# Batch 3's local q and k by DMA transposes instead of matrix transposes, with batch 4's loads reordered, in a fused sparse-attention and squared-ReLU kernel

## The chip, the cores and the metric

The kernel runs on one core of one Trainium2 chip. The time is device microseconds of one execution of the whole program. A core has five engines that run side by side, each in its own program order: TensorE (PE, matrix work), VectorE (DVE), ScalarE (ACT), GpSimd (POOL) and SyncE (SP). Here POOL mainly issues the loads from memory, which also convert float32 to bfloat16, and SP issues the stores and the transposes that DMA engines make.

## The reference

Eight batches of attention with 8 heads, 576 positions and 64 dimensions per head. Heads 0 to 3 see the last 32 positions ("local"), heads 4 to 7 see the positions of the same remainder modulo 32 ("strided"). The output, 4608 rows of 512, goes through a two-layer network.

```python
scores = scale * np.matmul(q, k.transpose(0, 1, 3, 2))
mask_local = (rel >= 0) & (rel < stride)                       # stride = 32
mask_strided = (rel >= 0) & (pos[None, :] % stride == pos[:, None] % stride)
masks = np.stack([mask_local if h < H // 2 else mask_strided for h in range(H)], axis=0)
scores = np.where(masks[None, :, :, :], scores, -1000000000.0)
attn = np.exp(scores - np.max(scores, axis=-1, keepdims=True))
attn = attn / (np.sum(attn, axis=-1, keepdims=True) + 1e-09)
attn_out = np.matmul(attn, v)
x = np.ascontiguousarray(attn_out.transpose(0, 2, 1, 3)).reshape(B * S, H * D)
out = np.square(np.maximum(x @ w_in, 0.0)) @ w_out
```

## The kernel before

**Tiles.** A unit is two heads of one batch, numbered 4 x batch + pair. Units 0 and 1 of a batch (so 12 and 13 for batch 3) are local, the other two strided. A local unit works on six tiles of 96 queries with 128 keys each, the 32 keys before the tile and its own 96. The attention result stands transposed in `xt` (four tiles of 128 x 4608). The network runs over nine chunks of 512 rows: first layer `mm1` (L709, 16 groups of four matmuls a chunk), relu on ScalarE (L715), square on VectorE (L716), second layer `mm2` (L731, 16 groups a chunk), copy to `y` (L735) and a store by SP (L739).

**Order.** The order is written by hand. The network's groups are numbered from 0, and `PLAN` lists, for each group, the steps of attention that are issued just ahead of it. Each engine takes its part of the steps in that order. Batch 3's attention is spread over groups 19 to 85, batch 4's over 40 to 121. Group 48 is the first of the second layer of chunk 1, group 64 the first of the first layer of chunk 2, group 80 the first of its second layer.

**Steps of the local units.** `l` loads the float32 rows of two units into the unused end of `xt` in one DMA (`load_qk_local_sw`, L292). `c` copies them into bfloat16 tiles `q_l`, `k_l` (L299), on the engine that the last letter names (v VectorE, a ScalarE). `T` makes six transposes on TensorE into PSUM (L455) and copies them out (L462). `Q` instead loads one unit's rows straight into `q_l` or `k_l`, one DMA per head (`load_qk_rows`, L280), and `Y` transposes q and k with two DMA transposes on SP (`transpose_local`, L380). Before, batches 0 to 3 go by `l`, `c`, `T` (batch 0 by loads of its own), batches 4 to 7 by `Q`, `Y`. `S` (with `!`, all at once) makes the scores, four exponentials on ScalarE (L523) and two masks on VectorE (L529), the first mask one group later, the second two. `D` multiplies by V, one head per part (L669), and divides on VectorE (L674, L675). `E` transposes the result into `xt`, from batch 2 on by DMA on SP (L684). From batch 4 on both local units' scores are made together by `G` (L552, exponentials L563, masks L559).

**V of the local units.** `V` loads it (`load_v_local_all`, L420): 128 partitions, of which the first 32 hold the last 32 rows of the tile before, so that those rows are loaded twice. For batch 0 `load_v_local_sw` (L405) loads the 96 own rows alone and `H` (`shift_v_local`, L412) copies partitions 96 to 127 to 0 to 31 of the next tile.

**Steps of the strided units.** `C` loads q or k (L351) into one staging tile for each of the two names; `X` transposes it by DMA on SP (L356) into `qT_s` (two buffers) or `kT_s` (one buffer). `k` copies `kT_s` into the block-diagonal `kb` (L367, L370), `U` loads V (L392, L395), `B` copies it into the block-diagonal `vb` (L399). `s` makes scores (L576), exponentials (L577) and a mask (L579); `x` the row sums (L587) and products (L590), a logarithm and an exponential for the reciprocal (L592, L593), and the products on VectorE into `xt` (L600; L606 for the third part).

**Queues.** All loads above stand in POOL's one queue, all DMA transposes and stores in SP's; an instruction there that waits holds up what stands behind it. The staging tile of `C` is free again when its `X` has landed.

Of the kernel before, what the change touches and what calls it, by code (L numbers as in the profile page):

```python
# [38 lines left out]
19: C2q C2k V2 k11v D4.0  # L39
20: s1.0 D4.1 B10v  # L40
21: s1.1 D5.0
22: B11v l3k12+13 s1.2 U2
23: D5.1 x1.0
24: E4a
25: x1.1
26: X2k l3q12+13
27: x1.2
28: V3 E5a
29: c9kv
30: c8qv  # L50
31: c8ka c9qv X2q
# [1 line left out]
35: T8kv  # L53
37: T9kv
38: T8qv C3k
41: S8!
42: T9qa
44: S9! D8.0 k20v
45: D8.1 k21v
46: B20v  # L60
47: E8 D9.0 B21v U3
48: Q16k s2.0
49: D9.1
50: Q17q Q16q c12kv s2.1
51: c12qa E9 s2.2
52: Q17k c13kv c13qa
54: x2.0
55: X3q X3k
56: x2.1 C4k C4q
57: T12ka  # L70
58: V4 T13qv T12qa
59: T13ka
60: x2.2 B30v
61: B31v
63: U4 S12!
64: X4q
65: D12.0
66: Y17 k30v
67: Y16 D12.1 S13! X4k C5q k31v
68: C5k  # L80
71: s3.0 E12 Q20k Q21q Q20q
72: Q21k s3.1
73: D13.0 D13.1
75: E13
77: s3.2
80: x3.0 B40v
81: B41v
82: x3.1
85: x3.2
90: G4 k40v  # L90
91: k41v
95: U5 D16.0 D16.1
97: Y20
99: X5k
100: C6k
101: X5q
# [62 lines left out]
def kernel(  # L159
# [136 lines left out]
    def cast_qk_local(u, name, copy):  # L296
        s = st[u]
        t = qk_in.tile([QL, 6, 2, D], BF16, name=f"{name}_l")
        copy(t.rearrange("p j h d -> p h j d"), s[name + "f"].rearrange("p h (j d) -> p h j d", j=6))  # L299
        s[name] = t  # L300
# [16 lines left out]
    def step_TS(b, name, g, copy):  # L317
        src = str_rows[b, name]
        pt = bank("pt").bitcast(BF16)[:, 0:S]
        if b:  # L320
            for i in range(NJ):
                c = 128 * (NJ * g + i)
                nc.tensor.transpose(pt[:, SP_ * i:SP_ * (i + 1)], src[:, c:c + 128], ident[0:SP_, 0:SP_])
            if g == 0:
                o = strTs[name].tile([128, NP2 * SR], BF16, name=f"{name}T_s")
                str_T[b, name] = o.rearrange("c (a p) -> c a p", p=SR)
            copy(str_T[b, name][:, NJ * g:NJ * (g + 1), 0:SP_], pt.rearrange("c (a p) -> c a p", p=SP_))
            return
        for i in range(2):
            for s3 in range(NP3):  # L330
                c = 128 * (2 * g + i)
                o = S // 2 * i + QL * s3
                nc.tensor.transpose(pt[:, o:o + QL], src[:, s3, c:c + 128], ident[0:QL, 0:QL])
        if g == 0:
            o = strTs[name].tile([128, 2 * NJ * SR], BF16, name=f"{name}T_s")
            str_T[b, name] = o[:, 0:2 * NJ * SP_].rearrange("c (a r) -> c a r", a=NJ // 2)
        o = str_T[b, name]
        copy(o[:, 2 * g:2 * g + 2, :].rearrange("c a r -> c (a r)"), pt)
        if g == 1:
            for i in range(2):  # L340
                st.setdefault(2 + i, {})[name + "T"] = \
                    o[:, :, 2 * SP_ * i:2 * SP_ * (i + 1)].rearrange("c a (h p) -> c h a p", h=2)
# [71 lines left out]
    def load_v_local_all(b):  # L414
        i = (2 * b) % NV
        t = vl_all[:, i:i + 2]
        src = v[b - 1:b + 1].rearrange("b h s d -> (b h s) d")
        r0 = H * S - 32
        src = bass.AP(src.tensor, src.offset + r0 * D, [[D, 128], [QL * D, 4 * NL], [1, D]])
        nc.gpsimd.dma_start(out=t[:, :, :, :, 0:D].rearrange("p u h t d -> p (u h t) d"), in_=src)  # L420
        for u in range(2):
            st.setdefault(4 * b + u, {})["v"] = t[:, u]
# [27 lines left out]
    def step_T(u, name, copy):  # L450
        s = st[u]
        src = s[name].rearrange("p j h d -> p (j h d)")
        pt = bank("pt").bitcast(BF16)[:, 0:S]
        for j in range(6):
            nc.tensor.transpose(pt[:, QL * j:QL * (j + 1)], src[:, 128 * j:128 * (j + 1)],  # L455
                                ident[0:QL, 0:QL])
        if name == "k":
            full = kTl[v_slot(u)]
            dst = full[:, 32:32 + S]
        else:  # L460
            full = dst = qkT.tile([128, S], BF16, name="qT")
        copy(dst.rearrange("c (p j) -> c p j", j=6), pt.rearrange("c (j p) -> c p j", j=6))  # L462
        s[name + "T"] = full
# [79 lines left out]
    def step_G(b):  # L543

        us = (4 * b, 4 * b + 1)
        bk = [bank("pt") for _ in range(6)]
        bk = [bk[0::2], bk[1::2]]
        for t in range(2 * NL):
            for row in range(2):
                s, j = st[us[t // NL]], t % NL  # L550
                rows, c = slice(64 * row, 64 * row + 64), QL * (t % 4)
                nc.tensor.matmul(bk[row][t // 4][:, c:c + QL], s["kT"][rows, QL * j:QL * j + 128],  # L552
                                 s["qT"][rows, QL * j:QL * (j + 1)], start=True, stop=True)
        e = es01[:, 0:4 * S].rearrange("p (r c) -> p r c", r=2)

        def masks(row):
            x = e[:, row].rearrange("p (u t c) -> p u t c", u=2, c=QL)
            for i in range(2):
                nc.vector.tensor_tensor(x[:, i], x[:, i], mask_all, op=ALU.mult)  # L559

        for row in range(2):
            for i in range(3):
                nc.scalar.activation(e[:, row, 4 * QL * i:4 * QL * (i + 1)], bk[row][i][:, 0:4 * QL], AF.Exp, scale=scale)  # L563
            later(row + 2, lambda row=row: masks(row), ("G", b, row))
# [197 lines left out]
    def warm(n):  # L762
        if n:
            pw = bank("py")
            for _ in range(n):
                nc.tensor.matmul(pw, idle[:, 0:128], idle, start=True, stop=True)
# [7 lines left out]
    def run_step(word):  # L774
        word, _, at = word.partition("/")
        places[:] = [int(x) for x in at.split(",") if x]
        op, arg = word[0], word[1:]
        if op == "w":
            warm(int(arg))
        elif op == "c":  # L780
            cast_qk_local(int(arg[:-2]), arg[-2], ENG[arg[-1]])
        elif op == "T":
            step_T(int(arg[:-2]), arg[-2], ENG[arg[-1]])
        elif op == "W":
            step_TS(int(arg[0]), arg[1], int(arg[2]), ENG[arg[3]])
        elif op == "S":
            u, _, half = arg.rstrip("!").partition(".")
            step_S(int(u), int("!" in arg), [int(half)] if half else range(2))
        elif op == "G":
            step_G(int(arg))  # L790
        elif op == "b":
            step_B(*(int(x) for x in arg.split(".")))
        elif op == "N":
            step_N(int(arg))
        elif op == "O":
            step_O(int(arg))
        elif op in "sx":
            (step_SS if op == "s" else step_XX)(*(int(x) for x in arg.split(".")))
        elif op == "k":
            step_K(int(arg[0]), int(arg[1]), ENG[arg[2]])  # L800
        elif op == "m":
            memset_later(arg[:-1], nc.gpsimd if arg[-1] == "g" else nc.vector)
        elif op == "D":
            if "." in arg:
                u, part = arg.split(".")
                step_D(int(u), int(part))
            else:
                step_D0(int(arg))
        elif op == "E":
            step_E(int(arg.rstrip("av")), ENG.get(arg[-1]))  # L810
        elif op == "P":
            first_part(*([int(x) for x in y] for y in arg.split(".")))
        elif op == "H":
            shift_v_local(int(arg[:-1]), ENG[arg[-1]])
        elif op == "C":
            load_str_tall(int(arg[:-1]), arg[-1])
        elif op == "Q":
            load_qk_rows(int(arg[:-1]), arg[-1])
        elif op == "X":
            transpose_str(int(arg[:-1]), arg[-1])  # L820
        elif op == "Y":
            transpose_local(int(arg))
        elif op == "V":
            load_v_local_all(int(arg))
        elif op == "U":
            load_v_str(int(arg))
        elif op == "B":
            spread_v_str(int(arg[0]), int(arg[1]), ENG[arg[2]])
        elif op == "l":
            load_qk_local_sw(int(arg[0]), [int(x) for x in arg[2:].split("+")], arg[1])  # L830
        elif op == "r":
            load_str_rows(int(arg[0]), arg[1])
        elif op == "i":
            load_w_in(int(arg))
        elif op == "o":
            load_w_out(int(arg))
        elif op == "z":
            late_constants()
        else:
            raise ValueError(word)  # L840
# [143 lines left out]
```

## Time and profile before

| | us |
|---|---|
| median of 3 runs (301.0 to 301.94) | 301.18 |
| profiled execution | 300.84 |
| its span, first to last instruction | 299.1 |
| TensorE busy in the span | 292.6 |
| VectorE, ScalarE, GpSimd busy | 178.5, 172.7, 72.5 |
| granted TensorE clock | 1.00 throughout |

The page of the profile gives the busy time of each engine and its share over 40 slices of the span. The timeline lists instructions in order of time, those of one form that follow each other merged: start, length, engine, line, operation, what it writes and reads, how many, and in brackets how long the engine was idle before and what ended that. For SP the length is the time that it took to issue; a transfer lands later. The view of a tile or line gives the shortest, median and longest duration. The costliest groups are these (busy us, mean ns of one, idle time of the engine before them):

```profile
L709 PE MATMUL psb<-xt,w_in_b 128*128 128x512 bf16 x576 | 133.7, 379 | 0.8 <-ACT xt L694 0.4
L731 PE MATMUL psb<-w_out_b,g_sb 128*128 128x512 bf16 x560 | 128.2, 379 | 0.0
L715 ACT ACTIVATE r<-psb 128x512 bf16<-128x512 f32 x144 | 85.4, 599 | 38.2 <-PE psb L709 34.7
L716 DVE TENSOR_TENSOR g_sb<-r 128x512 bf16<-128x512 bf16 x144 | 60.9, 424 | 75.5 <-ACT r L715 74.6
```

### The profile page before, as it was taken

How to read it: one execution, taken by the hardware profiler on the slowest of the kernel's cores; microseconds unless marked ns; L12 is line 12 of the kernel's file. 1: busy time of each engine (PE TensorE's matmuls, PEld its weight loads, DVE VectorE, ACT ScalarE, POOL GpSimd, SP SyncE). 2: the span in 40 equal slices, each digit the busy share in tenths (PEclk: the TensorE clock that was granted, in tenths of full speed). 3: DMA queues.
4: the chain of work that ended last, by engine and by line, in shares of the span. 5: the costliest groups of instructions: out<-in, count | busy, mean ns of one | idle time of the engine just before them, and what ended most of it. 6: DMA issues, size and time to landing. Idle time of an engine off the chain costs nothing.

```text
span 299.1 us, 5688 instructions
## 1 busy us (share of the span) xinstructions
PE 292.6 (98%) x2172; PEld 146.4 (49%) x2172; DVE 178.5 (60%) x460; ACT 172.7 (58%) x325; POOL 72.5 (24%) x105
## 2 busy tenths in 40 slices
PE   7989999999999999999999999999999999999996
PEld 3654555545545445444454445444454444444444
DVE  5857699569678695589257945685485525104400
ACT  3758855786668744773467546645665356126511
POOL 8746743004604009056303720000000000000000
PEclk9999999999999999999999999999999999999999
DMA  7999999999999999999998998611011110010012
GB/s 148 189 210 202 184 200 189 153 227 110 144 141 192 171 161 190 151 153 135 192 174 141 159 188 136 110 56 71 35 23 44 67 51 0 35 72 36 0 70 72
DMA packets 93132, 37.28 MB, mean 125 GB/s; under 512 B 78957, under 2 KB 87239, under 8 KB 93105
## 3 DMA queue, kind: packets, MB, share of 16 engines
q0 software_dynamic: 54448, 18.82, 60.3%
q1 hardware_dynamic: 38512, 18.03, 31.6%
q8 instruction: 17, 0.28, 0.4%
q14 instruction: 11, 0.08, 0.1%
q10 hardware_dynamic: 144, 0.07, 0.1%
HBM read 38.21 MB, written 9.44 MB: 159 GB/s over the span
## 4 chain that ended last, share of the span: by engine, by line
PE 88%; ACT 4%; DMA 2%; DVE 2%; issue 2%; POOL 0%; DVEq 0%; ACTq 0%; POOLq 0%
PE psb L709 39%; PE psb L731 39%; DMA w_out_b<-in_k_dram 2%; PE psb L669 2%; PE psb L590 1%; ACT r L715 1%; PE psb L756 1%; PE psb L576 1%; PE psb L587 1%; ACT e L511 1%; PE psb L455 1%; PE psb L552 1%; PE psb L507 1%; DVE vb L399 1%; ACT qT L462 0%
## 5 line engine op out<-in xcount | busy, mean ns | idle before, releaser
L709 PE MATMUL psb<-xt,w_in_b 128*128 128x512 bf16 x576 | 133.7, 379 | 0.8 <-ACT xt L694 0.4
L731 PE MATMUL psb<-w_out_b,g_sb 128*128 128x512 bf16 x560 | 128.2, 379 | 0.0
L715 ACT ACTIVATE r<-psb 128x512 bf16<-128x512 f32 x144 | 85.4, 599 | 38.2 <-PE psb L709 34.7
L716 DVE TENSOR_TENSOR g_sb<-r 128x512 bf16<-128x512 bf16 x144 | 60.9, 424 | 75.5 <-ACT r L715 74.6
L709 PEld LDWEIGHTS <-w_in_b 128*128 128x128 bf16 x576 | 53.4, 98 | 59.3 <-issue 2.1
L731 PEld LDWEIGHTS <-g_sb 128*128 128x128 bf16 x560 | 51.7, 97 | 57.1 <-DVE g_sb L716 0.3
L735 ACT COPY y<-psb 128x512 f32<-128x512 f32 x35 | 20.7, 590 | 53.6 <-PE psb L731 53.5
L600 DVE TENSOR_TENSOR xt<-psb,rv 64x144 bf16<-64x144 f32 x84 | 34.1, 406 | 7.8 <-ACT rv L593 6.7
L592 ACT ACTIVATE rv<-psb 128x432 f32<-128x432 f32 (+1 forms) x21 | 10.5, 500 | 10.4 <-PE psb L587 10.4
L675 DVE TENSOR_TENSOR x_l<-psb,rinv 96x384 bf16<-96x384 f32 x28 | 15.5, 554 | 1.0
L351 POOL DMA_DIRECT2D q_t<-in_q_dram x6 | 3.4, 567 | 44.9 <-DMA qT_s<-q_t 42.7
L606 DVE TENSOR_TENSOR xt<-psb,rv 64x270 bf16<-64x270 f32 (+1 forms) x28 | 10.9, 432 | 3.7 <-ACT rv L593 3.5
L577 ACT ACTIVATE e<-psb 128x432 bf16<-128x432 f32 (+1 forms) x21 | 10.4, 496 | 3.7 <-PE psb L576 3.7
L280 POOL DMA_DIRECT2D k_l<-in_k_dram x16 | 11.9, 746 | 2.2 <-ACT rv L593 1.9
L420 POOL DMA_DIRECT2D vl<-in_v_dram x7 | 10.3, 1474 | 7.6 <-PE psb L552 3.7
L280 POOL DMA_DIRECT2D q_l<-in_q_dram x16 | 11.8, 742 | 0.0
L563 ACT ACTIVATE e<-psb 128x384 bf16<-128x384 f32 x24 | 9.6, 509 | 3.4 <-PE psb L552 3.4
L593 ACT ACTIVATE rv<-rv 128x432 f32<-128x432 f32 (+1 forms) x21 | 11.2, 533 | 0.7
L669 PEld LDWEIGHTS <-e 128*128 128x128 bf16 x168 | 8.6, 101 | 4.8
L559 DVE TENSOR_TENSOR e<-e,mask_all 128x576 bf16<-128x576 bf16 x16 | 6.7, 459 | 6.9 <-ACT e L563 6.8
L351 POOL DMA_DIRECT2D k_t<-in_k_dram x6 | 3.2, 538 | 28.0 <-DMA kT_s<-k_t 25.8
L669 PE MATMUL psb<-vl,e 128*128 128x65 bf16 x168 | 9.5, 195 | 0.0
(117 smaller groups left out, 217.4 us busy)
## 6 DMA issues: line engine op xcount, KB each, us to landing
out_dram<-y SPq DMA_DIRECT2D x35, 256.0 KB, 2.8
vl<-in_v_dram POOLq DMA_DIRECT2D x7, 384.0 KB, 11.4
w_out_b<-in_moe_w_out_dram POOLq DMA_DIRECT2D x4, 512.0 KB, 14.3
q_t<-in_q_dram POOLq DMA_DIRECT2D x7, 288.0 KB, 6.4
k_t<-in_k_dram POOLq DMA_DIRECT2D x7, 288.0 KB, 6.6
v_st<-in_v_dram POOLq DMA_DIRECT2D x7, 216.0 KB, 8.3
w_in_b<-in_moe_w_in_dram POOLq DMA_DIRECT2D x2, 704.0 KB, 14.0
k_l<-in_k_dram POOLq DMA_DIRECT2D x16, 72.0 KB, 7.1
```

The source lines that it names most:

```text
L280: nc.gpsimd.dma_start(out=t[:, :, hh, :], in_=src[b, 2 * p + hh].rearrange("(t p) d -> p t d", p=QL))
L592: nc.scalar.activation(rv, pn, AF.Ln)
L593: nc.scalar.activation(rv, rv, AF.Exp, scale=-1.0)
L600: nc.vector.tensor_tensor(to[:, :, NJ * part:NJ * (part + 1), par], of, by, op=ALU.mult)
L606: nc.vector.tensor_tensor(t, of[:, g:, :, lo:lo + k], by[:, g:, :, lo:lo + k], op=ALU.mult)
L669: nc.tensor.matmul(po[0:m, n, :], e[:, c:c + m], rhs[:, NL * part + n, 0:D + 1], start=True, stop=True)
L675: nc.vector.tensor_tensor(x, po[0:QL, :, 0:D], rinv[0:QL].to_broadcast([QL, NL, D]), op=ALU.mult)
L709: nc.tensor.matmul(ph, w_in_b[:, kk, 128 * ff:128 * (ff + 1)], xt[kk][:, 512 * c:512 * (c + 1)], start=(kk == order[0]), stop=(kk == order ...
L715: nc.scalar.activation(r, ph, AF.Relu)
L716: later(1, lambda: nc.vector.tensor_tensor(g[:, ff, :], r, r, op=ALU.mult))
L731: nc.tensor.matmul(py, g[:, ff, 128 * j:128 * (j + 1)], w_out_b[:, ff, :], start=(ff == 0), stop=(ff == 15))
L735: nc.scalar.copy(y, py)
```

## The change

Four things are edited in the plan, and one in the step that carries out `V`.

1. Units 12 and 13: `l3k12+13` and `l3q12+13` become `Q12k Q13k` and `Q12q Q13q` in the same places (22, 26); the casts at 50 to 52 and the `T` steps at 57 to 59 are gone; `Y12` comes at 40 and `Y13` at 52.
2. Batch 4: `Q16` and `Q17` move from 48 to 52 to 56, between the strided loads; `X4k` goes ahead of `Y17` and `Y16`; V4 and U4 move from 58 and 63 to 67, behind `C5q`.
3. V of batches 3 and 4 is loaded by `load_v_local_sw`, 96 partitions, and `H3v`, `H4v` copy the shared rows on VectorE.
4. Batch 3's strided steps s3, x3, k30v, k31v come up to two groups later, B40v and B41v move from 80 and 81 to 97 and 98.

```diff
-22: B11v l3k12+13 s1.2 U2
+22: B11v Q12k Q13k s1.2 U2
-26: X2k l3q12+13
+26: X2k Q12q Q13q
-28: V3 E5a
+28: E5a V3
+40: Y12
-48: Q16k s2.0
+48: s2.0
-50: Q17q Q16q c12kv s2.1
-51: c12qa E9 s2.2
-52: Q17k c13kv c13qa
+50: s2.1
+51: E9 s2.2
+52: Y13
-56: x2.1 C4k C4q
-57: T12ka
-58: V4 T13qv T12qa
-59: T13ka
+56: x2.1 C4q Q16k Q16q C4k Q17k Q17q
 60: x2.2 B30v
 61: B31v
-63: U4 S12!
+62: H3v
+63: S12!
 64: X4q
 65: D12.0
-66: Y17 k30v
-67: Y16 D12.1 S13! X4k C5q k31v
-68: C5k
-71: s3.0 E12 Q20k Q21q Q20q
-72: Q21k s3.1
-73: D13.0 D13.1
-75: E13
-77: s3.2
-80: x3.0 B40v
-81: B41v
-82: x3.1
+66: X4k Y17
+67: D12.1 S13! Y16 C5q V4 U4
+68: k30v
+69: k31v C5k
+71: E12 Q20k Q21q Q20q
+72: Q21k
+73: D13.0 D13.1 s3.0
+75: E13 s3.1
+78: s3.2
+81: x3.0
+83: x3.1
 85: x3.2
+94: H4v
 95: U5 D16.0 D16.1
-97: Y20
+97: Y20 B40v
+98: B41v
...
         elif op == "V":
-            load_v_local_all(int(arg))
+            (load_v_local_sw if int(arg) in (3, 4) else load_v_local_all)(int(arg))
```

The functions that it now calls for batches 3 and 4 stood in the kernel already:

```python
def load_v_local_sw(b):
    i = (2 * b) % NV
    t = vl_all[:, i:i + 2]
    nc.gpsimd.dma_start(out=t[32:128, :, :, :, 0:D].rearrange("p u h t d -> p (u h t) d"),
                        in_=v[b, 0:4].rearrange("h (t p) d -> p (h t) d", p=QL))

def shift_v_local(b, copy):
    t = vl_all[:, (2 * b) % NV:(2 * b) % NV + 2].rearrange("p u h t d -> p (u h) t d")
    copy(t[0:32, :, 1:NL, 0:D], t[96:128, :, 0:NL - 1, 0:D])
```

All other steps keep their places. Line numbers after the plan move by one.

## The prediction

> **What bounds the kernel now.** I read the page first: busy times, then slices.
>
> ```profile
> PE 292.6 (98%) x2172; PEld 146.4 (49%) x2172; DVE 178.5 (60%) x460; ACT 172.7 (58%) x325; POOL 72.5 (24%) x105
> PE   7989999999999999999999999999999999999996
> ```
>
> TensorE is full from the second slice to the last. Then who it waits for (view of waits, TensorE): 3.2 us in all, of which two lie after 20 us, one of 0.2 on ScalarE at 91.6 and this one.
>
> ```profile
> PE psb L590 <- DVE vb L399: 0.5, 1, 0.5
> ```
>
> So a change pays by matrix work removed, and costs by any wait it puts in front of TensorE. Off-path work counts only where it reaches TensorE. The timeline of TensorE shows what is removed:
>
> ```profile
> 77.99 1.02 PE L731 MATMUL psb<-w_out_b,g_sb 128*128 128x512 bf16 x4
> 78.85 0.42 PE L455 MATMUL psb<-ident,k_l 96*128 96x96 bf16 x6
> 79.11 1.03 PE L731 MATMUL psb<-w_out_b,g_sb 128*128 128x512 bf16 x4
> 79.98 0.68 PE L455 MATMUL psb<-ident,q_l 96*128 96x96 bf16 x12
> 80.49 1.03 PE L731 MATMUL psb<-w_out_b,g_sb 128*128 128x512 bf16 x4
> 81.35 0.42 PE L455 MATMUL psb<-ident,k_l 96*128 96x96 bf16 x6
> 81.61 1.03 PE L731 MATMUL psb<-w_out_b,g_sb 128*128 128x512 bf16 x4
> ```
>
> The reader is to see starts, not durations: matmuls overlap in the pipeline, so a row's length overstates its price. From 78.85 to 79.11 is 0.26 us for six transposes, 79.98 to 80.49 is 0.51 for twelve.
>
> **Removed.** Units 12 and 13 lose T12k, T12q, T13k, T13q: 24 transposes, 0.26 + 0.51 + 0.26 = **1.03 us on the path**. Their four copies out of PSUM (0.64 us each on ScalarE, 0.76 on VectorE) and four casts (0.82 on ScalarE, 0.35 on VectorE) go too. TensorE waited for none of them here, so they count nothing.
>
> **Added: Y12, Y13.** Four transposes on SP's queue. They take 1.21 us of SP each at 100 to 105 us and land in 2.6 to 5.6; the slowest transpose of the loaded stretch took 11.3 (the strided k at 78.71) and 4.67 of SP (56.04). Y12 comes after the store issued at 60.76, so even at 2 x 4.67 + 11.3 it lands by about 78; S12 wants it at 84.4 (85.46 less 1.03): covered by 6 us. Y13 comes after the store at 74.97 and before X3q, X3k. S13 wants it near 89. At 1.2 of SP each and 5 to 8 us to landing it is there at 82 to 85; at 4.33 and 11.3 it comes at 91, 2 us late. I take the first, since X3q and X3k were so slow beside the eight row loads of units 16 and 17, which the change puts behind X3q (C4q waits for it, and those loads follow on POOL).
>
> **Moved behind Y13: X3q, X3k.** These issues and the wait they feed:
>
> ```profile
> 75.60 3.02 SPq L356 DMA_TRANSPOSE qT_s<-q_t  x1
> 78.71 4.33 SPq L356 DMA_TRANSPOSE kT_s<-k_t  x1
> 90.53 0.55 POOL L351 DMA_DIRECT2D k_t<-in_k_dram  x1 [9.15 <-DMA kT_s<-k_t]
> ```
>
> X3k landed at 90.0 and k30v ran at once; the change gives k30v and k31v one and two groups more. X3k would be issued 2.4 us later (two at 1.2), at 81.1, and land between 6 us after (the same transpose at 105.26 landed at 111.3) and 11.3: 87 to 92.4. I take 88, below k30v's new place of about 89.5, so nothing. The upper end is a rival.
>
> **Batch 4's loads.** X4k goes ahead of Y17 and Y16 and waits for k31v, as it must, since kT_s has one buffer; behind it stand Y17, Y16, E12, E13. Before, X4k left at 105.26, Y17 at 99.99, E12 at 106.74. Now X4k can leave when k31v is done, near 92, and the rest follow. C5q waits only for X4q, and V4, U4 stand behind it on POOL: some 97 us (C4q issued at 84, X4q after its landing at 90, 6 us more) against 92.1 before; with the 8.5 us that V4 took to land, it is there at about 106. H4v is at plan 94, near 116: 10 us of cover.
>
> **Loads of units 12, 13.** Two 288 KB loads become eight of 72 KB, 0.73 us of POOL each instead of 0.7 for four of them. U2 and V3 are issued at least 4.4 us later for it (8 x 0.73 less 2 x 0.7); V3 landed near 68.6, B30 to H3v come after 84. V3 and V4 shrink from 384 to 288 KB. Nothing on the path, except where POOL's issues meet VectorE's copies (third rival).
>
> **Added: H3v, H4v.** The only earlier one took 484 ns:
>
> ```profile
> L412 DVE COPY vl<-vl x1: 484/484/484, 12.8 to 12.8; 32x1280 bf16<-32x1280 bf16 x1
> 84.14 1.57 DVE L606 TENSOR_TENSOR xt<-psb,rv 64x270 bf16<-64x270 f32 x4 [1.29 <-ACT rv L593]
> 85.75 1.05 DVE L399 COPY vb<-v_st 54x1408 bf16<-54x1408 bf16 x2
> 86.83 0.83 DVE L529 TENSOR_TENSOR e<-e,mask_all 128x576 bf16<-128x576 bf16 x2
> 87.56 0.36 PE L669 MATMUL psb<-vl,e 128*128 128x65 bf16 x6
> ```
>
> VectorE runs without a gap from x2.2's products (L606, held to 84.14 by ScalarE) over B30v, B31v (L399) to the two masks of S12; the exponentials that they need began at 85.79 and the first two were done by 86.5, so the copies set the mask's start. The first mask ends at 87.29 (86.83 + 0.46), and D12.0 on TensorE reads it at 87.56. H3v stands between B31v and that mask: 0.48 + 0.02 between instructions moves its end to 87.79. From VectorE's end to the matmul are 0.06 us (L399 ends at 43.83, the waiting L590 starts at 43.89), so D12.0 starts at 87.85 instead of 87.56: **0.29 us of new wait**. TensorE works in order, so all behind it moves. Between zero (the copy out of the way) and 0.55 (no slack at all) I take 0.29. H4v has cover: the last mask of G4 ends at 115.55 and D16.0 starts at 117.22.
>
> **s3, x3, B40v, B41v.** Scores a group or two later, products x3.0 and x3.1 one later, B40v and B41v (0.52 each) out of VectorE's unbroken run from 104.3 to 112.05 that ends just before G4 at 112.28. One group is 0.86, the two copies 1.05: this run ends about 0.2 earlier. No gain, no loss.
>
> **Sum.** Span 299.1 - 1.03 + 0.29 = 298.36; the profiled run took 300.84, so 1.74 lies around the span: 300.10. It stood 0.34 below the median 301.18, which gives **300.45** on the median.
>
> **Rivals.** About 0.3% (0.9 us) is what a measurement here can tell from no change: 300.28 and 302.08 are the borders.
>
> *The whole 1.03 comes.* H3v's wait does not appear: the ScalarE result that starts x2.2's products comes earlier, now that its copies of T13 are gone. For it: 1.29 us of VectorE idle before L606. Against: the copy of y and the logarithm on that chain waited for TensorE itself. 301.18 - 1.03 = 300.15.
>
> *Slower: the strided k of batch 3 comes late.* Y13 takes slots of up to 4.33 us each ahead of X3k and it keeps its 11.3: issue at up to 87.4, landing 98.7. k30v then stops VectorE, and behind it stands the second mask of S13, which D13.1 wants near 94.8. From landing to that matmul are k30v's two copies (0.53 together), the mask (0.46) and 0.06: about 1.1. So it costs from 93.7 on, one for one; slower than before from 94.4, and by 0.9 from 95.3. In the middle of the bad stretch (96.2) the wait is 2.5: 301.18 - 0.74 + 2.5 = 302.9. Against: 68 to 92 us held the unit 16 and 17 loads, which now wait.
>
> *POOL's issues stretch the copies.* C4q and those eight loads are now issued from X3q's landing on (issue near 78, 6 us to landing: 84 to 92), over B30v, B31v, H3v; before, POOL was quiet from 81.4 to 90.5. What that can do:
>
> ```profile
> L399 DVE COPY vb<-v_st x14: 510/521/1061, 41.0 to 193.4; 54x1408 bf16<-54x1408 bf16 x14
> 40.26 1.44 POOL L420 DMA_DIRECT2D vl<-in_v_dram  x1 [0.41 <-DMA v_st<-in_v_dram]
> ```
>
> The 1061 ns copy started at 40.96, inside that issue. All three stretched so: 3 x 0.54 = 1.62, or 302.07. But of five L399 under an issue one doubled, one grew by 0.09 and three did not; at half a stretch, 0.8, it is 301.25. The same meeting at B11v (43.31) could add up to 0.27 there. The Trainium skill ("SBUF — State Buffer", the two sides of SBUF) calls the pair of ports that VectorE and GpSimd share an exclusive lock: whoever starts second waits for the whole instruction of the first. By that rule each copy that begins under a 0.73 us row-load issue waits for its end, up to 302.6 with three; the three undisturbed rows speak against it as it stands.
>
> **Chances.** The forecast 0.45 (its own range 300.0 to 300.9: faster 0.15, same 0.30). The whole gain 0.27 (faster 0.23, same 0.04). Late k 0.14 (slower 0.13, same 0.01). Stretched copies 0.14 (same 0.09, slower 0.05). Together: faster 0.38, same 0.44, slower 0.18. The range, 299.8 to 301.9, takes in the first two and most of the stretched copies, and leaves out the late k.
>
> **What would show it.** No L455 rows after 75 us and the rows of L731 there back to back, 1.03 less. A wait of TensorE at D12.0 for the mask, about 0.3, with H3v just ahead of it on VectorE. DMA landings of X3k below 89. L399 at 86 us at 0.52 says no stretch. Wrong would be a wait elsewhere in 40 to 120 us: at S12 or S13 for their transposes, or at D13.1.

## The result, and the profile after

The changed kernel took 310.93 us (median of 6 runs, 308.06 to 311.43), the kernel before 300.63 beside it (6 runs, 300.16 to 301.94): ratio 1.0327, interval 1.0302 to 1.0352. It is slower by 3.3%. Ratios leave out executions over 1.5% longer than the fastest of their kernel, which the medians include, so the two can point to different sides. The profiled execution took 311.43 us, its span is 309.5 (before 299.1): 10.4 us to account for.

The page of the changed kernel, TensorE's busy time and the slices of TensorE and of its granted clock:

```profile
PE 290.9 (94%) x2112; PEld 145.7 (47%) x2148; DVE 178.6 (58%) x459; ACT 169.8 (55%) x320; POOL 76.3 (25%) x111
...
PE   7899989999999954999999999999999999999995
...
PEclk9999999999999995999999999999999999999999
```

A slice is 7.7 us. Before, all slices but the first, the third and the last stood at 9; now the 15th and 16th (108 to 124 us) are half empty, and the clock is low in the 16th. The view of waits of the changed kernel, TensorE (us in total, times, longest):

```profile
PE psb L553 <- DMA kTl<-k_l: 8.2, 1, 8.2
...
PE psb L591 <- DVE vb L400: 0.9, 1, 0.9
PE psb L670 <- DVE e L530: 0.6, 1, 0.6
```

One row has nearly all of it: the scores of G4 (L553; L552 before) wait for a DMA transpose, the k of unit 16 (Y16). The row of L591 was 0.5 before; the row of L670 (D12.0) is new. The timeline of TensorE at the first row:

```profile
120.61 1.14 PE L553 MATMUL psb<-qT,kTl 64*128 64x96 bf16 x24 [8.25 <-DMA kTl<-k_l]
121.69 4.49 PE L732 MATMUL psb<-w_out_b,g_sb 128*128 128x512 bf16 x14
```

In the stretch without waits shown in the prediction, these matmuls started every 0.216 us: 14 of them would take 13 x 0.216 + 0.38 = 3.19. These 14, the ones that start before 126 us, where the view ends, took 4.49. So the idle time is followed by 1.3 us lost to slow matmuls. The windows of the changed kernel show why (stretch, its length, busy time and count of PE, PEld, DVE, ACT, POOL, then granted clock, DMA share, GB/s):

```profile
108.00:112.00 4.00, 3.95 (x21) 1.76 (x18) 3.87 (x11) 1.43 (x3) 0.00 (x0) 1.00 2.32 91
112.00:116.00 4.00, 0.36 (x1) 0.00 (x0) 0.61 (x3) 0.00 (x0) 0.73 (x1) 1.00 1.59 83
116.00:120.00 4.00, 0.00 (x0) 0.00 (x0) 0.00 (x0) 0.00 (x0) 2.17 (x3) 0.69 1.94 110
120.00:124.00 4.00, 3.39 (x30) 1.80 (x31) 1.64 (x4) 2.40 (x6) 0.00 (x0) 0.50 1.70 207
```

The clock is down to 0.50 when TensorE resumes. The last two columns are the other reading: the DMA engines are busy all through the stretch and move little. The kernel before, 108 to 112 us:

```profile
108.00:112.00 4.00, 4.00 (x21) 1.75 (x18) 3.89 (x10) 1.41 (x3) 0.19 (x1) 1.00 1.26 208
```

Nearly twice the share (2.32 against 1.26) for less than half the rate (91 against 208 GB/s). What was under way there, from the view of DMA of the changed kernel for issues between 99.3 and 106.5 us (last number: median us from issue to landing):

```profile
vl<-in_v_dram POOLq DMA_DIRECT2D x1, 288.0 KB, 14.4
k_t<-in_k_dram POOLq DMA_DIRECT2D x1, 288.0 KB, 16.0
v_st<-in_v_dram POOLq DMA_DIRECT2D x1, 216.0 KB, 14.5
...
qT<-q_l SPq DMA_TRANSPOSE x2, 11.4
kTl<-k_l SPq DMA_TRANSPOSE x2, 15.9
```

and of the kernel before, issues between 100 and 104 us, where these four transposes stood nearly alone (132 packets of loads in these 4 us):

```profile
qT<-q_l SPq DMA_TRANSPOSE x2, 3.3
kTl<-k_l SPq DMA_TRANSPOSE x2, 4.5
```

V4, U4, C5k and the first rows of unit 20 went out together with Y17 and Y16, and the transposes took 3.5 times as long (11.4 against 3.3, 15.9 against 4.5), V4 1.7 times (14.4 against 8.5).

**Where 10.4 us went.** The weight loads of the two layers come in the same number and order in both traces, so their starts can be compared one by one. The changed kernel is 0.2 us ahead up to 43 us. It loses 0.46 at B11v (L591), gains 1.03 between 79 and 82 us, where the transposes are gone, and loses 0.80 at D12.0 (the view of waits has 0.62, since it counts from the modelled end of the matmul before). G4 starts 8.3 later for its wait, and slow matmuls cost another 1.8, 0.5 of it in G4's own scores. That makes 10.1, and from 118 us of the kernel before to its last weight load this distance doesn't change. The last 0.3 lie behind the last matmul.

### The profile page after: what moved, and what is told of

It reads as the page before. It is cut to its first block, busy times and chain, and to the rows that moved or that the text cites. A ratio compares the mean times of both kernels' runs of the same rounds, so it can differ in the third digit from the quotient of the medians.

```text
span 309.5 us, 5615 instructions
## 1 busy us (share of the span) xinstructions
PE 290.9 (94%) x2112; PEld 145.7 (47%) x2148; DVE 178.6 (58%) x459; ACT 169.8 (55%) x320; POOL 76.3 (25%) x111
## 4 chain that ended last, share of the span: by engine, by line
PE 72%; DMA 14%; DVE 4%; issue 3%; SPq 2%; ACT 2%; POOL 2%; POOLq 0%; DVEq 0%; ACTq 0%
PE psb L710 33%; PE psb L732 31%; DMA kTl<-k_l 5%; DMA w_in_b<-in_moe_w_in_dram 3%; DMA q_l<-in_q_dram 2%; SPq L381 2%; DMA q_t<-in_q_dram 2%; DMA qT_s<-q_t 2%; ACT r L716 1%; PE psb L757 1%; PE psb L670 1%; PE psb L591 1%; DVE vb L400 1%; PE psb L553 1%; PE psb L577 1%
## 5 line engine op out<-in xcount | busy, mean ns | idle before, releaser
L710 PE MATMUL psb<-xt,w_in_b 128*128 128x512 bf16 x558 | 132.1, 379 | 1.7 <-DMA w_in_b<-in_moe_w_in_dram 0.5
L732 PE MATMUL psb<-w_out_b,g_sb 128*128 128x512 bf16 x542 | 126.9, 382 | 1.0 <-issue 0.2
L281 POOL DMA_DIRECT2D q_l<-in_q_dram x20 | 14.7, 739 | 13.5 <-DMA vl<-in_v_dram 10.5
L281 POOL DMA_DIRECT2D k_l<-in_k_dram x20 | 14.8, 746 | 4.7 <-DMA w_out_b<-in_moe_w_out_dram 2.3
L560 DVE TENSOR_TENSOR e<-e,mask_all 128x576 bf16<-128x576 bf16 x16 | 6.7, 458 | 15.9 <-ACT e L564 15.9
L578 ACT ACTIVATE e<-psb 128x432 bf16<-128x432 f32 (+1 forms) x21 | 10.4, 496 | 4.2 <-PE psb L577 3.7
L670 PEld LDWEIGHTS <-e 128*128 128x128 bf16 x168 | 8.5, 101 | 5.7 <-DVE e L530 1.1
L553 PE MATMUL psb<-qT,kTl 64*128 64x96 bf16 x96 | 3.2, 222 | 8.2 <-DMA kTl<-k_l 8.2
L670 PE MATMUL psb<-vl,e 128*128 128x65 bf16 x168 | 9.5, 195 | 0.6 <-DVE e L530 0.6
L591 PEld LDWEIGHTS <-vb 128*128 128x128 bf16 x154 | 7.1, 97 | 4.9 <-DVE vb L400 1.2
```

The source lines that it names most:

```text
L281: nc.gpsimd.dma_start(out=t[:, :, hh, :], in_=src[b, 2 * p + hh].rearrange("(t p) d -> p t d", p=QL))
L670: nc.tensor.matmul(po[0:m, n, :], e[:, c:c + m], rhs[:, NL * part + n, 0:D + 1], start=True, stop=True)
L710: nc.tensor.matmul(ph, w_in_b[:, kk, 128 * ff:128 * (ff + 1)], xt[kk][:, 512 * c:512 * (c + 1)], start=(kk == order[0]), stop=(kk == order ...
L732: nc.tensor.matmul(py, g[:, ff, 128 * j:128 * (j + 1)], w_out_b[:, ff, :], start=(ff == 0), stop=(ff == 15))
```

## The experiments

All kernels below compute the whole reference. A plan line of the diffs is a step list of the kernel.

### Which step of the order made the collision

In the changed plan C5q stands ahead of V4 and U4 on POOL and waits for the landing of X4q (99.06), so nothing behind it leaves before 99.6. Four kernels change only that order. The first puts both ahead:

```diff
-67: D12.1 S13! Y16 C5q V4 U4
+67: D12.1 S13! Y16 V4 U4 C5q
```

> The changed kernel with V4 and U4 ahead of C5q on POOL instead of behind it. Theory (order of POOL's queue): C5q waits for X4q's landing, so V4 and U4 behind it leave at 100 to 102 us and run beside Y17, Y16 and E12, and all of them slow each other; ahead of C5q they leave near 92.5 and 94, Y16's k lands by 108 and G4's wait of 8.25 us goes: 300.5 to 301.5. Rival (the DMA engines have more work than they can do, from the extra transposes and row loads): the order changes nothing, G4 still waits 6 us or more, 308 or more.

Measured 303.85 us (10 runs, 300.95 to 313.32), ratio 1.0066 [1.0028, 1.0104]. The waits of this kernel, TensorE:

```profile
PE psb L553 <- DMA kTl<-k_l: 1.9, 1, 1.9
```

V4 and U4 now left at 92 to 94 and landed at 103 to 107; Y16's k landed at 113.24 (120.57 in the changed kernel), 5.84 after its issue, but the issue came at 107.40 instead of 104.35. One step's place gives back 6.3 of 8.2 us of the wait and 2.6 of 3.3%. The theory had asked for more, a landing by 108 and 300.5 to 301.5 us; its rival, no change, is ruled out.

The next three, each by itself: V4 alone ahead (e2), U4 alone ahead (e3), C5k behind the row loads (e4).

```diff
-67: D12.1 S13! Y16 C5q V4 U4
+67: D12.1 S13! Y16 V4 C5q U4
```

```diff
-67: D12.1 S13! Y16 C5q V4 U4
+67: D12.1 S13! Y16 U4 C5q V4
```

```diff
-69: k31v C5k
+69: k31v
-72: Q21k
+72: Q21k C5k
```

> Only V4 ahead of C5q, U4 stays behind. If V4's many 128-byte rows are what slows the transposes: G4's wait falls below 2 us, about 301 to 302.5. If U4's long rows (4096 bytes) are: it stays above 4 us, 305 or more. If it is the sum of the loads in flight: in between, 3 to 6 us of wait.

> Only U4 ahead of C5q, V4 stays behind. If U4's long rows slow the transposes: G4's wait falls below 2 us, about 301 to 302.5. If V4's short rows do: above 4 us, 305 or more. If it is the sum of the loads in flight: in between.

> C5k behind Q20 and Q21 on POOL instead of ahead of them, V4 and U4 as in the changed kernel. If the next batch's strided k, now loaded early, is what fills the DMA engines at 103 to 118 us: G4's wait falls by 3 us or more. If V4 and U4 are: it stays within 2 us of 8.25, 308 to 311.

V4 alone ahead: 308.94 us, ratio 1.0248 [1.0212, 1.0285]. U4 alone: 309.32, 1.0243 [1.0179, 1.0307]. C5k behind the row loads: 309.38, 1.0277 [1.0236, 1.0318], G4's wait 5.0 in an execution of 308.01. By these ratios each load taken away gives back 0.5 to 0.8%, V4 and U4 together 2.6; the intervals of U4 and C5k still touch the changed kernel's (1.0302 to 1.0352). No one of them is the whole cause. Each of the three kernels still leaves U4 or C5k, or both, beside the transposes.

Is the order enough by itself? The next kernel is the one before, with V4 and U4 behind C5q and nothing else changed:

```diff
-58: V4 T13qv T12qa
+58: T13qv T12qa
-63: U4 S12!
+63: S12!
-67: Y16 D12.1 S13! X4k C5q k31v
+67: Y16 D12.1 S13! X4k C5q V4 U4 k31v
```

> The kernel before with one thing moved: V4 and U4 behind C5q on POOL. Nothing is added or removed. Theory (loads that run beside Y17 and Y16 slow them): V4 and U4 leave at 104.5 beside Y16's k and X4k; X4k or Y16's k lands 3 to 8 us later than its 109.6 and 111.3, with a wait at G4 or at D16 for V4 of 2 to 8 us: 303 to 309. Rival (only together with the extra transposes): 301, no wait.

Measured 315.34 us (314.76 to 316.81), ratio 1.0509 [1.0484, 1.0534]: worse than the whole change and than the 303 to 309 that was expected. Waits of TensorE, and the row of VectorE's timeline that they go back to:

```profile
PE psb L552 <- DVE xt L600: 12.8, 1, 12.8
```

```profile
120.82 1.05 DVE L399 COPY vb<-v_st 54x1408 bf16<-54x1408 bf16 x2 [15.08 <-DMA v_st<-in_v_dram]
```

U4 was issued at 103.08 and landed at 118.4 and 120.8. B40v, at group 80 in that plan, held VectorE 15 us for it, and the products of x3 that free G4's PSUM banks stand behind. The collision needs no new transposes: the loads behind C5q meet the ones that were always there. The victim differs: there U4, in the changed kernel Y16's k. In g3 Y16's k landed at 110.57, 8.4 after its issue and in time for G4. U4 was as late in the changed kernel (118.16), but its B40v stands behind G4. So the 5.1% are the price of this order in the plan of before, not a part of the 3.3%.

Next: which loads slow a transpose. This kernel leaves only short-row loads beside Y17 and Y16 (rows of 64 values) and takes the long-row ones away (U4, C5k: packets of 4096 bytes):

```diff
-67: D12.1 S13! Y16 C5q V4 U4
+67: D12.1 S13! Y16 U4 C5q V4
-69: k31v C5k
+69: k31v
-72: Q21k
+72: Q21k C5k
```

> The changed kernel with U4 ahead of C5q and C5k behind Q20, Q21: of the loads only V4, Q20 and Q21 are issued beside Y17 and Y16. Theory A (the loads with the strided rows, U4 and C5k, slow the transposes): Y16's k lands within 8 us of its issue, TensorE's wait at G4 for it is under 1 us (8.2 in the changed kernel), time 301 to 302.5. Theory B (any load in flight slows them, by the sum of the packets): landing 13 us or more after issue, the wait stays at 4 us or more, time 305 to 309.

Measured 305.8 us (305.45 to 307.6), ratio 1.0173 [1.0134, 1.0213]. The time lies in B's range, the wait (3.2) in neither's. Y16's k landed 7.9 us after its issue, which is A's number, but the issue came at 107.33 instead of 104.35: Y17 had to wait for the rows of unit 17, which landed at 103.16 (99.33 in the changed kernel) with U4 now in flight beside them. So the wait remained. Theory A is right about the rate, as packets show. First the kernel before, issues from 100 to 104 us; then this kernel, 108 to 114; then the changed kernel, 106 to 114 (packets of the stretch, MB, and their time as a share of 16 engines; q1 are the transposes, q0 the loads):

```profile
q1 hardware_dynamic: 2305, 0.57, 83.5%
q0 software_dynamic: 132, 0.09, 13.2%
```

```profile
q0 software_dynamic: 2858, 0.36, 98.1%
q1 hardware_dynamic: 2346, 0.57, 75.9%
```

```profile
q0 software_dynamic: 1046, 0.54, 143.6%
q1 hardware_dynamic: 671, 0.16, 47.2%
```

Transposes move 576 packets per us nearly alone (2305 in 4 us), 391 beside short rows (2346 in 6), 84 beside a mix with long rows (671 in 8). The changed kernel shows both by itself: from 118 us, when no 4096-byte packet is left, its transposes are back at 398 per us (1593 in 4).

```profile
q0 software_dynamic: 1706, 0.21, 87.9%
q1 hardware_dynamic: 1593, 0.39, 80.5%
```

Counted by size, the changed kernel moved from 106 to 116 us 823 packets of 256 bytes (transposes), 803 of 128 and 105 of 4096. The Trainium skill ("DMA: Bandwidth & Descriptors", Queues, rings and completion order) says that each DMA engine serves its queues in turn, one packet of each. The counts are in keeping with it: in the mixed stretches the loads move 1.1 to 1.6 packets for one of the transposes. They don't prove it, since equal counts can come about otherwise. That a turn is so dear when a few 4096-byte packets are about (690 ns each on average there; the six in the 4 us of the kernel before took 324) is measured here; why is open.

### What each part of the change costs alone

Part 1 alone in the kernel before (f1); f2 is the reverse, the changed kernel without part 1.

```diff
-22: B11v l3k12+13 s1.2 U2
+22: B11v Q12k Q13k s1.2 U2
-26: X2k l3q12+13
+26: X2k Q12q Q13q
+40: Y12
-50: Q17q Q16q c12kv s2.1
-51: c12qa E9 s2.2
-52: Q17k c13kv c13qa
+50: Q17q Q16q s2.1
+51: E9 s2.2
+52: Q17k Y13
-57: T12ka
-58: V4 T13qv T12qa
-59: T13ka
+58: V4
```

Part 3 alone in the kernel before (f3):

```diff
+62: H3v
+94: H4v
-            load_v_local_all(int(arg))
+            (load_v_local_sw if int(arg) in (3, 4) else load_v_local_all)(int(arg))
```

The changed kernel with the rows of units 16 and 17 in their old places (f4):

```diff
-48: s2.0
+48: Q16k s2.0
-50: s2.1
+50: Q17q Q16q s2.1
-52: Y13
+52: Q17k Y13
-56: x2.1 C4q Q16k Q16q C4k Q17k Q17q
+56: x2.1 C4q C4k
```

> The kernel before with part 1 of the change alone: units 12 and 13 by direct row loads and DMA transposes (Y12 at 40, Y13 at 52), batch 4's loads, V and the strided steps as before. Theory (the new order of batch 4's loads makes the wait): Y17, Y16 land by 112 as before, no wait at G4, 24 transposes less on TensorE: 1.0 us faster than before, unless Y13 ahead of X3q and X3k beside the eight row loads brings X3k after 94, which would show as a wait of D13 or s3. Rival (four more DMA transposes and smaller loads overload the DMA engines by themselves): a wait of several us at G4 here too, 304 or more.

> The changed kernel with part 1 undone: units 12 and 13 by one load, casts and transposes on TensorE as before; the order of batch 4's loads, V and the strided steps as changed. Theory (order): X3q now lands earlier, but C5q, V4, U4 still run beside Y17 and Y16, so a wait at G4 of 4 us or more stays, 305 or more. Rival (the extra transposes): the wait goes, 301 to 302.

> The kernel before with part 3 alone: V of batches 3 and 4 by 96 partitions, H3v at 62, H4v at 94. By the prediction's step D12.0 waits 0.3 us more for the mask behind H3v (no loads are issued there in this order, so the copies stay at 0.52), and V4 lands no later: 0.3 us slower than before. Rival: the smaller load frees the DMA engines and nothing waits: 0.

> The changed kernel with Q16 and Q17 back at 48 to 52, ahead of the strided loads of batch 4. Theory, in its narrow form (V4 and U4 behind C5q alone): no change, G4 waits 5 us or more. In its wide form (everything of batch 4 was pushed late behind X3q): Y17 goes right behind X4k at 95, its data being there, lands by 103, and Y16 with it: G4's wait falls below 2 us, 300.5 to 302.5. Rival (overload): X3k then lands after 94 beside the row loads, with waits at D13 or s3.

*f1:* 306.54 us (303.47 to 308.7), ratio 1.0137 [1.0035, 1.0240]: not faster, and too wide to say by how much it is slower. Its waits, TensorE:

```profile
PE psb L575 <- DVE kb L366: 2.1, 1, 2.1
...
PE psb L551 <- DMA kTl<-k_l: 1.2, 2, 0.7
PE psb L589 <- DVE vb L398: 0.8, 1, 0.8
```

L575 are the scores of s3: they wait for k30v and that for X3k, which landed at 93.10. This is the late strided k of the prediction's rival, not in the changed kernel but in part 1 without the rest, and on another path: the rival had D13.1 wait for S13's mask, and nothing for a landing before 93.7. That its 2.5 us come near the 2.1 is luck.

*f2:* 307.41 us (303.12 to 311.44), ratio 1.0121 [0.9985, 1.0257], too wide for a verdict between the theory's 305 or more and the rival's 301 to 302. In the profiled execution, the longest of the four, G4 waited 7.8 us for Y16's k without any Y12 or Y13; whether the others did isn't shown.

*f3:* 301.22 us (300.34 to 302.78), ratio 1.0006 [0.9977, 1.0035]: no difference. But the trace has the predicted wait. VectorE and TensorE, timelines of f3:

```profile
85.30 1.05 DVE L401 COPY vb<-v_st 54x1408 bf16<-54x1408 bf16 x2
86.38 0.48 DVE L414 COPY vl<-vl 32x1280 bf16<-32x1280 bf16 x1
86.90 0.83 DVE L531 TENSOR_TENSOR e<-e,mask_all 128x576 bf16<-128x576 bf16 x2
```

```profile
86.25 1.03 PE L711 MATMUL psb<-xt,w_in_b 128*128 128x512 bf16 x4
87.41 0.37 PE L671 MATMUL psb<-vl,e 128*128 128x65 bf16 x6
```

Four matmuls from 86.25 end their turn at 86.25 + 4 x 0.216 = 87.11; D12.0 (L671) starts at 87.41, 0.30 late. The time can't show it: the interval is 0.9 us to either side, and in the profiled execution the 0.5 wait at 43.9 was gone as well.

*f4:* 310.07 us (309.35 to 311.03), ratio 1.0290 [1.0219, 1.0362], G4's wait 8.1: where the rows of units 16 and 17 stand doesn't decide. It missed the wide form of the theory and fits the narrow one.

Then unit 12 alone by DMA, half of part 1, in the kernel before:

```diff
-22: B11v l3k12+13 s1.2 U2
+22: B11v Q12k l3k13 s1.2 U2
-26: X2k l3q12+13
+26: X2k Q12q l3q13
+40: Y12
-50: Q17q Q16q c12kv s2.1
-51: c12qa E9 s2.2
+50: Q17q Q16q s2.1
+51: E9 s2.2
-57: T12ka
-58: V4 T13qv T12qa
+58: V4 T13qv
```

> The kernel before with unit 12 alone by row loads and Y12, unit 13 as before. Y12 lands before E8 is issued and nothing later stands behind it: twelve transposes less, 0.5 us faster than before. If the DMA engines are so full that any addition makes batch 4 late: 0.5 us or more slower, with X3k or Y16's k later by 1 us or more.

300.6 us (12 runs, 300.03 to 308.67), ratio 1.0012 [0.9998, 1.0026]: the 0.51 us are gone again, 0.3 of it into L590's wait for vb (0.8; before 0.5), and T13 now waits 0.6 for its casts (L455 for q_l and k_l), which the kernel before doesn't.

### Is the gain there once the waits are gone?

Each kernel here takes away the wait that the one before it showed. g1 is f1 with Y17 and Y16 ahead of X4q; g5 adds part 3 with H3v earlier; h3 puts U2 ahead of the row loads on POOL; h4 does so for unit 12 alone; h5 moves B40v and B41v behind G4's masks; h6 also lets V4 and U4 leave earlier.

g1, against f1 (the steps s3, x3, k30v, k31v, B40v and B41v also stand one or two groups later):

```diff
-64: X4q
+64: Y17 Y16 X4q
-66: Y17 k30v
-67: Y16 D12.1 S13! X4k C5q k31v
-68: C5k
+67: D12.1 S13! C5q
+68: k30v
+69: k31v X4k C5k
...
```

g5, against g1:

```diff
+59: H3v
+94: H4v
-            load_v_local_all(int(arg))
+            (load_v_local_sw if int(arg) in (3, 4) else load_v_local_all)(int(arg))
```

h3, against g5; h4 makes the same swap in g4 (with l3k13 for Q13k) and takes over g5's edit:

```diff
-22: B11v Q12k Q13k s1.2 U2
+22: B11v s1.2 U2 Q12k Q13k
```

h5, against h3:

```diff
-81: x3.0 B40v
-82: B41v
+81: x3.0
+92: B40v
+93: B41v
```

h6, against h5:

```diff
-56: x2.1 C4k C4q
+56: x2.1
-63: U4 S12!
+63: U4 S12! C4k C4q
```

> Part 1 on the kernel before, with its order of batch 4's loads kept, but Y17 and Y16 on SP ahead of X4q (their rows land by 93, X4q's by 100), and s3, x3, k30v, k31v at their changed places. Theory (what runs together decides): Y16's k lands near 100 beside two strided loads at most, G4 waits for nothing, s3 comes after k31v without a wait: 0.7 to 1.0 us faster than before. Rival (the DMA engines are full whatever the order): X4k is then the late one, with 1 to 3 us of wait at G4's neighbours or s4, 302 or more.

> The same with V of batches 3 and 4 by 96 partitions, H3v moved from 62 to 59, where VectorE sat idle for 1.29 us, and H4v at 94. By the prediction's step the wait of D12.0 was H3v's place alone: no wait of TensorE for the mask of S12, time within 0.3 us of the run without it. If D12.0 still waits 0.3 us or more, the step was wrong.

g1: 303.79 us (302.78 to 308.13), ratio 1.0112 [1.0089, 1.0134]; Y16's k landed at 102.8, but G4 waited 2.1 us for products that stood behind B40v, and B40v for U4 (landed 108.9). Neither the theory nor its rival, a late X4k, had that. g5: 301.33 us (12 runs, 299.81 to 310.32), 1.0033 [1.0015, 1.0050]; in its profile, of the fastest execution, the only wait that the kernel before lacks is 1.0 at L591 (0.5 before). With H3v at group 59 the wait at D12.0 is gone, as expected. The time isn't within 0.3 us of g1's: U4 landed at 105.3 here, and G4 didn't wait for it.

> The version with local transposes first, V of batches 3 and 4 loaded without shared rows and H3v ahead of S12's masks, and now U2 (which waits for B11v's copies) ahead of the row loads Q12k and Q13k on POOL. Theory A (the row loads' issues stretch B11v): TensorE's wait for vb near 43.9 falls from 1.0 to 0.5 us or less, no other wait appears, and the time is 299.5 to 300.5, 0.3 to 0.8 below the kernel before less what the batch 4 loads cost in some executions. Rival: B11v is slow whatever POOL issues; the wait stays at 0.8 to 1.1 and the time at 301.

> The kernel before with unit 12 alone transposed by DMA (12 of the 24 transposes gone, 0.51 us), V of batches 3 and 4 loaded without shared rows with H3v ahead of S12's masks, and U2 ahead of Q12k and unit 13's load on POOL. Theory A: wait for vb 0.5 or less, no other new wait, 0.3 to 0.7 us faster than the kernel before. Rival: the wait at 43.9 stays at 0.8 to 1.0 and the time is the same as before (within 0.3).

h3: 302.36 us (299.69 to 305.87), ratio 1.0021 [0.9991, 1.0051]. Its waits, TensorE:

```profile
PE psb L553 <- DVE xt L607: 1.2, 1, 1.2
PE psb L553 <- DVE xt L601: 0.5, 1, 0.5
PE psb L591 <- DVE vb L400: 0.4, 1, 0.4
```

L591's wait fell from 1.0 to 0.4, theory A's number. But its reason isn't shown by that: in g5 B10v and B11v were not stretched, they took 0.52 us each and came late, because VectorE had waited 0.96 us for the load that B10v copies; in h3 it didn't wait, though B10v took 1.02. U4 landed at 107.7 this time (105.3 in g5), and the wait of g1 was back. h4: 300.87 us (299.63 to 306.87), ratio 0.9995 [0.9972, 1.0019], no difference.

> The version with U2 ahead of the row loads, and now B40v and B41v (which wait for U4's landing) behind G4's masks instead of between the products of batch 3. Theory A (those copies hold VectorE for a late U4, and G4 waits for the products behind them): no wait of TensorE at G4 for xt, the wait at 43.9 stays at 0.5 or less, and the time is 299.3 to 300.2, 0.3 to 1.0 below the kernel before. Rival (the wait only passes on, to Y16's k at G4 or to v in batch 4's sums): a wait of 0.5 us or more between 108 and 125 remains, time 300.5 to 302.

> The same, with V4 and U4 also ahead of C4k and C4q on POOL, so that they leave when B31v's copies are done (near 86) and not behind X3k's landing (near 92). Theory A (fewer loads beside Y17 and Y16): their k lands by 100 (104 to 107 before that), time as in the version with B40v behind G4 or up to 0.3 less. Rival (the loads now stand beside X3k, and k30v waits for it): X3k lands after 93 and TensorE waits 0.5 us or more at S13's or batch 3's scores, time 301 or more.

> The version with B40v and B41v behind G4's masks once more, for a profile of an ordinary run and a narrower ratio. Theory A (the 1.03 us are there once the waits are gone): no wait of TensorE at G4, D12.0 or 43.9 above 0.5 us, span 297.8 to 298.4, ratio below 1 by 0.1 to 0.4%. Rival (what is won is given back by executions in which the transposes run late): ratio within 0.1% of 1.

h5: 300.56 us (12 runs, 299.54 to 311.3), ratio 0.9987 [0.9963, 1.0011]; once more: 300.98 (12 runs, 299.31 to 307.72), 0.9991 [0.9963, 1.0019]. From the second of the two, a profile of an execution of 299.76 us:

```profile
core 0 of [0], span 297.9 us
...
PE psb L768 <- DVE xt L873: 1.3, 1, 1.3
PE psb L335 <- DMA w_out_b<-in_k_dram: 0.7, 1, 0.7
PE psb L509 <- DVE kTl L464: 0.4, 1, 0.4
```

No wait is left at G4, at D12.0 or at 43.9 us, and the span is 1.2 below the kernel before's 299.1. By the starts of the weight loads 1.03 of that is won between 78 and 82 us, and 0.4 is the wait at 43.9, which f3's execution lacked as well, without part 1; 0.3 is lost again behind the last matmul. So one execution has the gain; over all of them the two intervals hold 1, and no version was shown to be faster. The rival isn't ruled out either: 8 of h5's 24 executions took 305 us or more, of the 34 of the kernel before beside them 2 did. h6: 311.12 us (307.97 to 315.47), ratio 1.0377 [1.0328, 1.0427]. V4 left at 82.3 beside X3q, X3k and the rows of unit 17 and landed 22.9 us later, U4 20.9, Y16's k at 112.08 instead of 106.19: the rival's side, and by a worse price than it named. X3k, which it watched, landed at 93.92 and cost TensorE 1.0 (S13's mask 0.6, s3 0.4). The larger loss was at batch 4: VectorE stood 6.12 us for X4k ahead of G4's masks and H4v, and the products behind them waited 1.9 and 2.7. Here leaving earlier meant landing no earlier (V4 105.2, in h5 104.7).

## Why the prediction was wrong

**What failed: the step "Batch 4's loads".** It had V4 leave at some 97 and land at about 106, "with the 8.5 us that V4 took to land", and called it covered by 10 us to H4v. V4 left at 100.15 and landed at 114.57, 14.4 us later. The cover at H4v was indeed enough; the loss was elsewhere. The step says of X4k that it can leave near 92 "and the rest follow", and gives that rest (Y17, Y16, E12, E13) no landing times. They didn't follow: X4k left at 95.18, but Y17 only at 99.38, when the rows of unit 17 had landed (99.33), so Y17 and Y16 left no earlier than before (99.99) and met the loads (changed kernel, SP):

```profile
95.18 1.26 SPq L357 DMA_TRANSPOSE kT_s<-k_t  x1
99.38 1.80 SPq L381 DMA_TRANSPOSE qT<-q_l  x1
```

Y16's k among them is what G4 waits for. Before, it was issued at 103.93 and landed at 109.55, 2.7 us ahead of G4 at 112.28; now it was issued at 104.35 and landed at 120.57. The one duration of the step was taken from a stretch in which loads and transposes hardly met, while the change moved them into each other. e1 shows that undoing this order gives back 2.6 of 3.3%, g3 that in the plan of before it makes the loads late without any new transpose. The prediction also wrote down the number that warned of it: X3q and X3k "were so slow beside the eight row loads", 11.3 us. It used that for the place that the rows left and didn't ask it of the place that V4, U4 and C5k went to. At 11.3 after its issue Y16's k would have been due at 115.65, 3.4 us late.

**Removed, 1.03 us: right.** The matmuls of the second layer stand back to back there, with no L455 between them (changed kernel, TensorE), and those behind start 1.03 us earlier against the kernel before than those ahead. In h5's execution it is the same 1.03.

```profile
78.67 3.18 PE L732 MATMUL psb<-w_out_b,g_sb 128*128 128x512 bf16 x13
```

**H3v's wait, 0.29 us: right as long as POOL issues nothing beside it.** Alone (f3) it is 0.30. In the changed kernel, counted the same way, it was 0.79 (four matmuls from 85.91 end their turn at 86.77, D12.0 starts at 87.56), for the reason of the third rival: POOL's issues lay over the copies (changed kernel, VectorE; then f4, in which POOL issues nothing from 81 to 90 us):

```profile
84.96 1.33 DVE L400 COPY vb<-v_st 54x1408 bf16<-54x1408 bf16 x2
86.32 0.69 DVE L413 COPY vl<-vl 32x1280 bf16<-32x1280 bf16 x1
```

```profile
84.30 1.05 DVE L400 COPY vb<-v_st 54x1408 bf16<-54x1408 bf16 x2
85.39 0.48 DVE L413 COPY vl<-vl 32x1280 bf16<-32x1280 bf16 x1
```

1.33 instead of 1.05 and 0.69 instead of 0.48 are 0.49 more, and 0.79 - 0.30 = 0.49 reached TensorE. In f4 D12.0 is 0.31 late. The rival's half stretch was 0.8.

**B11v, up to 0.27 us: too small.** L591's wait rose by 0.4. In this trace B10v took 1.34 us (before 1.06) and B11v 0.70 (0.52), 0.46 more, so the stretch accounts for it; but in g5 the same wait came from a late load, so the rise isn't shown to have one cause. The exclusive lock of the Trainium skill, weighed in the prediction ("SBUF — State Buffer", the two sides of SBUF), isn't seen as it stands: in e1 two copies that began at 84.29, under C4q's issue of 84.16 to 84.92, took 1.06 as without one, and it was the issue that grew, to 0.76 from 0.52 in the changed kernel.

**Y12, Y13, X3q, X3k: right.** The transposes of Y13 landed by 83.0, X3k at 86.18 (forecast 88), C4q left at 84.6 (84). The late strided k is real in f1 (X3k at 93.10, wait 2.1): the rows of units 16 and 17, where they stood before, collide with Y13 and X3k. Part 2 of the change cures that and makes the collision at 100 us instead.

**The rivals** held no case of the transposes of batch 4, though TensorE waits for them at G4; rivals were looked for at 43 us and between 84 and 95, where the change adds transfers and copies, not at 100 to 112, where it only moves them.

## What to carry to other kernels

When a plan moves a DMA, draw which transfers will be in flight together and price every one of them at the slowest landing that the trace has for such a meeting, not at its own calm row. In an in-order queue, look first at what the moved step now stands behind: one load that waits (C5q for X4q's landing) turned four spread loads into a burst. A cover holds only against the crowded price: G4's 2.7 us were enough for a landing 5.6 us after issue and nothing for one of 16.2.

## What the runs showed that was not expected

A wait of TensorE can cost more than its length. In the kernel with short rows only, a wait of 3.2 us was followed by matmuls at half pace (timeline and windows of that kernel):

```profile
115.28 1.07 PE L553 MATMUL psb<-qT,kTl 64*128 64x96 bf16 x24 [3.19 <-DMA kTl<-k_l]
116.29 5.72 PE L732 MATMUL psb<-w_out_b,g_sb 128*128 128x512 bf16 x20
```

```profile
116.00:118.00 2.00, 2.00 (x15) 0.76 (x10) 1.04 (x3) 2.00 (x6) 0.00 (x0) 0.50 1.22 123
```

Twenty at 0.216 us apart take 19 x 0.216 + 0.38 = 4.48; 5.72 is 1.24 more. In h3 two waits of 0.45 and 1.25 us within 2.5 us were followed by the same (20 in 6.09 us, 1.6 more), while two of 0.90 and 1.25 in g1 and one of 1.95 in e1 were not (20 in 4.49). The Trainium skill ("TensorE: Matmul & The Clock Gate", What's actually happening) states a half clock after an idle window of some 3.4 us and full speed after as long a busy one. The length of the slow stretch agrees: in the short-row kernel the windows of 2 us around it were granted 0.85, 0.50 and 0.80, which is 0.6 + 2.0 + 0.8 = 3.4 us at half clock; the same sum over 116 to 126 us of the changed kernel is 6.8, twice that. Its start does not, at least in h3: there it came after less than 2 us of waiting in a stretch of 2.5.

The other surprise is the transposes' rate: 576 packets per us nearly alone, 391 beside short-row loads, 84 beside a mix with 4096-byte packets, at a DMA share that goes up, not down. A busy DMA share with few GB/s is how such a stretch looks in the windows.
